# A fused attention and two-layer MoE kernel: the opening stretch put into a written order, with its loads on three queues

## The chip, the core and the metric

The kernel runs on one core of a Trainium2 chip. The metric is device time in microseconds (us), taken as the median of several executions of the compiled program. Before the change three runs gave 962.1, 963.79 and 965.07 us.

## What is computed

Attention, then a feed-forward layer with PReLU, then one with a rational function. The heads 0 to 3 look back 32 positions, the heads 4 to 7 look back 128 in steps of 4:

```python
batch, n_heads, seq, head_dim = (4, 8, 576, 64)
mask_plain = (rel >= 0) & (rel < window)                      # window = 32
mask_dil = (rel >= 0) & (rel < window * dilation) & (rel % dilation == 0)   # 4
scores = np.where(masks[None, :, :, :], scale * (q @ k.T), -1000000000.0)
attn = np.exp(scores - np.max(scores, axis=-1, keepdims=True))
attn = attn / (np.sum(attn, axis=-1, keepdims=True) + 1e-09)
x = attn @ v                                  # 2304 tokens x 512
h = x @ w_in                                  # 512 x 2048
x = (np.maximum(h, 0) + alpha * np.minimum(h, 0)) @ w_out     # 2048 x 512
h = x @ w_in2
P = a[0] + a[1]*h + a[2]*h*h + a[3]*h*h*h
Q = 1.0 + np.abs(b[0]) * np.abs(h) + np.abs(b[1]) * h*h
out = (P / (Q + 1e-06)) @ w_out2
```

The weights of the first layer reach the kernel as 64-bit floating point numbers, read as pairs of 32-bit words.

## The kernel before

The tokens go through the attention and the first layer in eight chunks of 288 (`u` = 0 to 7). A chunk has four attention jobs, one for each pair of heads `hp`: 0 and 1 plain, 2 and 3 dilated. A job is a Python generator; each `next` issues one of its steps. In order: load q and k; transpose them on PE into `pq` and `pk` (L382, L386); copy these to `qT` and `kT` on ACT (L392, L393); load v; scores `ps` on PE (L435 plain, L423 dilated); masked row maxima on DVE (L449), in two groups of blocks; exponentials with row sums on ACT (L457); normalize on DVE (L464, L465, L467); transpose the probabilities on PE into `pp` (L478); copy them to `pT` on ACT (L484); multiply with v into `px` (L529); copy to the layer's input `x1f` (L541).

The first layer runs, for each chunk, in 16 steps of 128 hidden features: `h` (L668 for the first 8 steps of chunk 0, in plain fp32; L551 for the rest, in three passes over a high and a low half), the PReLU on ACT and DVE (L685, L688, L691), which needs `side` and `salpha` made from `alpha` at L629 to L634, and the second product `y` (L716, L725). The trace's `h0`, `h1`, ... below are the steps 0, 1, ... of chunk 0.

The weights are decoded from their 64-bit form by turns. A turn loads a block of w_in and, from turn 2 on, one of w_out into one of two `raw` buffers (`w64_load`, L134 and L139; the turns 0 and 1 bring w_in alone), turns the exponent on ACT (L148), then sign, upper and lower part on DVE (L154, L161, L168; the last once for w_in and once for w_out). With two buffers the load of turn n waits for the decoding of turn n-2.

What stands ahead of the steady loop is the head: the four jobs of chunk 0, the first turns, and PE's warm-up matmuls (L606). The string `HEAD` lists it, one character a step: a digit is the next step of that job (0 to 3 counts in the order of `HPS`, so job 0 of the string is pair 1), `d`, `x`, `J`, `i`, `h`, `l` are the stages of the decoding, `k` starts the first job of chunk 1. The scheduler is free to choose another order within it. After it, attention jobs of the later chunks are put at fixed half steps of the loop, and `PACE` says how many turns of decoding each step takes along. Loads are issued by SP, in its program's order; `alpha`, `a` and `b` by POOL. An fp32 matmul leaves two records in the trace, so that a step `h` of four matmuls counts x8. In the rows a job of chunk 0 has the name `hd`, and later ones `tq`, `tk`, `tv`, `pr`, `pT`.

Of the kernel before, what the change touches and what calls it, by code (L numbers as in the profile page):

```python
# [22 lines left out]
def tile_attention_moe_moe2(  # L23
# [48 lines left out]
    HEAD = '0d12d30011xj01Ji223301h2300110011xj22223333Jil001101d22010331hlxj220133Ji012301d23k0123hl23xj2323Jidhl'  # L72
# [3 lines left out]
    MANH = ''  # L76
    HPS = (1, 0, 3, 2)
    POOLJ = ()
    SPLIT = True
# [7 lines left out]
    PACE = ((8, 0.75), (16, 0.25), (24, 0.75), (128, 0.22))  # L87
# [190 lines left out]
    def mem_head(nm, dil):  # L278

        if dil:  # L280
            at = {"tq": (0, 0), "tk": (0, 512), "tv": (1, 0), "qT": (1, 512),
                  "kT": (2, 0), "pT": (2, 416), "pr": (3, 0)}
        else:
            at = {"tq": (0, 0), "qT": (0, 384), "tv": (1, 0), "kT": (1, 640),
                  "tk": (2, 0), "pr": (2, 512), "pT": (3, 0)}
# [22 lines left out]
    def attention_job(mem, u, hp, bk, eng=nc.sync, split=False):  # L308
# [5 lines left out]
        first = t0 == 0  # L314
        if dil:
            nb, bq = 4, C1 // 4
            kw = bq if first else bq + W
# [3 lines left out]
            tk = mem("tk", [kw, 2, 4 * D])  # L321

            def load(t, src, back):
                n = t.shape[0]
                s0 = t0 if not back or first else t0 - 4 * W
                eng.dma_start(
                    t,
                    src[b, h0 : h0 + 2, s0 : s0 + 4 * n, :].rearrange(
                        "h (i r) d -> i h (r d)", r=4
                    ),  # L330
                )

            load(tq, q, False)
            load(tk, k, True)

            duo = lambda t, j: t[:, j // 2, (j % 2) * 2 * D : (j % 2 + 1) * 2 * D]
            q_rows, k_rows = bq, kw
        else:


            nb, bq = 3, 96
            groups = ((0, 1, 2), (3, 4))
            rows, span = P, 96
            back = 0 if first else W
            key = [max(0, QS * j - W + back) for j in range(5)]
            k_rows = 96 if first else 80
            nk = (C1 + back) // k_rows
            tq = mem("tq", [bq, nb, 2, D])
            tk = mem("tk", [k_rows, nk, 2, D])

            def load(t, src, s0, step, n):
                for h in range(2):
                    eng.dma_start(
                        t[:, :n, h, :],
                        bass.AP(
                            src.tensor, ((b * H + h0 + h) * S + s0) * D,
                            [[D, t.shape[0]], [step * D, n], [1, D]],
# [3 lines left out]
            def load_one(t, src, s0):  # L361

                eng.dma_start(
                    t,
                    bass.AP(
                        src.tensor, ((b * H + h0) * S + s0) * D,
                        [[D, t.shape[0]], [S * D, 2], [1, D]],
                    ),
                )

            load(tq, q, t0, bq, nb)
            load(tk, k, t0 - back, k_rows, nk)

            duo = lambda t, j: t[:, j].rearrange("p h d -> p (h d)")
            q_rows = bq
# [4 lines left out]
        kn = 4 if dil else nk  # L380
        for j in range(nb):
            nc.tensor.transpose(  # L382
                pq[:, j * q_rows : (j + 1) * q_rows], duo(tq, j), ident[:q_rows, :q_rows]
            )
        for j in range(kn):
            nc.tensor.transpose(  # L386
                pk[:, j * k_rows : (j + 1) * k_rows], duo(tk, j), ident[:k_rows, :k_rows]
            )
        yield
        kT = mem("kT", [P, kn * k_rows])  # L390
        qT = mem("qT", [P, C1])
        nc.scalar.activation(qT, pq[:, :C1], AF.Copy)  # L392
        nc.scalar.activation(kT, pk[:, : kn * k_rows], AF.Copy)  # L393
        yield
        if dil:
            tv = mem("tv", [kw, 2, 4 * D])
            load(tv, v, True)
        else:
            tv = mem("tv", [span, 5, 2, D])
            s0 = t0 - back  # L400
            if first:
                load_one(tv[:, 0], v, s0)
                load(tv[:, 1:], v, s0 + key[1], QS, 4)
            else:
                load(tv, v, s0, QS, 5)
# [8 lines left out]
        def scores():  # L414


            if dil:

                ps[:] = [bk(f"ps{nm}_{g}") for g in range(2)]
                for c in range(nb):  # L420
# [41 lines left out]
        def norm(gs):  # L462
            s = slice(groups[gs[0]][0], groups[gs[-1]][-1] + 1)
            nc.vector.tensor_scalar_add(sm[:, s], sm[:, s], 1e-9)  # L464
            nc.vector.reciprocal(sm[:, s], sm[:, s])  # L465
            n = s.stop - s.start
            (nc.vector if u < NORM_DVE else nc.gpsimd).tensor_tensor(  # L467
                pr[:, s], pr[:, s],
                sm[:, s].unsqueeze(2).to_broadcast([rows, n, span]), op=ALU.mult,
# [13 lines left out]
        def turned(g):  # L483
            nc.scalar.activation(  # L484
                pT[:, g * width[0] : g * width[0] + width[g]], pp[g][:span, : width[g]],
                AF.Copy,
            )
# [10 lines left out]
        if split:  # L498
            norm((0,))
            yield  # L500
# [3 lines left out]
        if split:  # L504
            turn(0)
            yield
            turned(0)
            yield
        rest = (1,) if split else (0, 1)
        norm(rest)  # L510
        yield
        for g in rest:
            turn(g)
        yield
        for g in rest:
# [539 lines left out]
```

## Time and profile before

| what | value |
|---|---|
| median of 3 runs | 963.79 us (962.1 to 965.07) |
| profiled execution | 964.02 us, of which span 962.2 us |
| mean granted clock of TensorE | 0.983 of full |
| PE busy | 936.0 us (97%) |
| DVE, ACT, POOL busy | 663.7 (69%), 631.8 (66%), 212.9 (22%) us |
| chain that ended last | PE 85%, DMA 5%, ACT 5%, DVE 3% |

The span is what the profiler saw from the first instruction to the last; the execution's own time is 1.8 us longer. PE is TensorE's matmuls, and PEclk its granted clock as a share of full speed, so 0.50 is the lower of its two levels (1.2 of 2.4 GHz). "Idle before" is the time an engine stood still just ahead of an instruction, and the name behind the arrow is what released it.

### The profile page before, as it was taken

To read this page: it belongs to the slowest core of one execution; us is meant where nothing else is said; L and a number is where in the kernel's file an instruction comes from. 1 tells how busy PE (TensorE), PEld (TensorE's weight loads), DVE (VectorE), ACT (ScalarE), POOL (GpSimd) and SP (SyncE) were. 2 spreads that over 40 slices of the span, in tenths; PEclk is the share of its full clock that TensorE was granted. 3 is DMA by queue.
4 is the path that set the end of the run, shared out by engine and by line. 5 is a ranking of instruction groups with operands and counts; after the bars stand their busy time and mean duration, and the time that the engine had idled before them with its cause. 6 is when DMAs were issued, how large, how long until landed. Compare 5 with 4: busy or idle time off the path is not lost.

```text
span 962.2 us, 18305 instructions
## 1 busy us (share of the span) xinstructions
PE 936.0 (97%) x6640; PEld 865.9 (90%) x6640; DVE 663.7 (69%) x1578; ACT 631.8 (66%) x1579; POOL 212.9 (22%) x257
## 2 busy tenths in 40 slices
PE   5899999999999999999999999999999999999998
PEld 5577998999999999999999999999999999999996
DVE  3688996556556555655536688877777777777776
ACT  3787676665564565555636588777776767767775
POOL 2000000010000010000013345443343343343332
PEclk7699999999999999999999999999999999999999
DMA  7655544463543544534144422021030020020000
GB/s 179 170 179 167 167 133 152 144 185 101 185 123 107 180 131 119 158 109 132 47 132 159 153 72 66 1 72 28 1 99 1 33 66 1 34 66 1 34 1 33
DMA packets 93898, 94.39 MB, mean 98 GB/s; under 512 B 40176, under 2 KB 81648, under 8 KB 93808
## 3 DMA queue, kind: packets, MB, share of 16 engines
q1 hardware_dynamic: 87360, 83.78, 28.5%
q0 software_dynamic: 6448, 9.45, 4.0%
q8 instruction: 52, 0.85, 0.4%
q14 instruction: 38, 0.31, 0.1%
HBM read 69.48 MB, written 23.72 MB: 97 GB/s over the span
## 4 chain that ended last, share of the span: by engine, by line
PE 85%; DMA 5%; ACT 5%; DVE 3%; issue 1%; SPq 0%; POOL 0%; POOLq 0%; ACTq 0%; DVEq 0%
PE h L551 39%; PE o L968 20%; PE y L725 17%; PE px L529 2%; DMA raw<-in_moe_w_out_dram 2%; DMA raw<-in_moe_w_in_dram 2%; PE pp L478 1%; PE ps L435 1%; PE h L668 1%; DMA hd<-in_q_dram 1%; PE ps L423 1%; ACT pr L457 1%; ACT hd L457 1%; PE y L716 1%; DMA x2hi<-y_0h 1%
## 5 line engine op out<-in xcount | busy, mean ns | idle before, releaser
L551 PE MATMUL h<-x1h,wl 128*128 128x288 f32 x480 | 147.2, 307 | 0.6 <-DVE g_9l L694 0.6
L551 PE MATMUL h<-x1l,wh 128*128 128x288 f32 x480 | 142.5, 297 | 0.0
L551 PE MATMUL h<-x1h,wh 128*128 128x288 f32 x480 | 142.0, 296 | 0.0
L688 DVE SCALAR_TENSOR_TENSOR h<-h,salpha,r 128x288 f32<-128x288 f32 x128 | 66.9, 523 | 95.2 <-ACT r L685 95.2
L551 PE MATMUL h<-x2h,wl 128*128 128x384 f32 x384 | 130.4, 340 | 0.0
L551 PE MATMUL h<-x2h,wh 128*128 128x384 f32 x384 | 130.0, 339 | 0.0
L551 PE MATMUL h<-x2l,wh 128*128 128x384 f32 x384 | 129.6, 338 | 0.0
L467 POOL TENSOR_TENSOR pr<-pr,sm 128x480 f32<-128x480 f32 (+2 forms) x20 | 23.9, 1197 | 453.4 <-DVE sm L465 384.7
L685 ACT ACTIVATE r<-h,side 128x288 f32<-128x288 f32 x128 | 63.7, 498 | 91.3 <-PE h L551 88.4
L900 POOL TENSOR_SCALAR qq<-hh,babs 128x384 f32<-128x384 f32 x96 | 56.7, 590 | 225.1 <-ACT hh L898 225.0
L903 POOL TENSOR_TENSOR qq<-qq,w 128x384 f32<-128x384 f32 x96 | 97.8, 1019 | 8.3 <-POOL qq L900 0.5
L551 PEld LDWEIGHTS h<-x1h,wl 128*128 128x128 f32 x480 | 90.5, 189 | 3.2 <-DVE g_9l L694 0.7
L551 PEld LDWEIGHTS h<-x1l,wh 128*128 128x128 f32 x480 | 90.8, 189 | 0.4 <-DVE x1l L543 0.2
L551 PEld LDWEIGHTS h<-x1h,wh 128*128 128x128 f32 x480 | 90.7, 189 | 0.1
L898 ACT ACTIVATE hh<-h 128x384 f32<-128x384 f32 x96 | 47.0, 490 | 62.6 <-PE h L551 62.6
L905 DVE TENSOR_TENSOR t<-h,t 128x384 f32<-128x384 f32 x96 | 53.5, 557 | 47.6 <-ACT t L904 47.1
L551 PEld LDWEIGHTS h<-x2h,wl 128*128 128x128 f32 x384 | 72.0, 188 | 4.0
L551 PEld LDWEIGHTS h<-x2l,wh 128*128 128x128 f32 x384 | 72.1, 188 | 3.6
L914 ACT ACTIVATE w<-qq 128x384 f32<-128x384 f32 (+1 forms) x98 | 50.8, 519 | 33.7 <-POOL qq L903 33.6
L551 PEld LDWEIGHTS h<-x2h,wh 128*128 128x128 f32 x384 | 72.0, 187 | 0.0
L922 DVE TENSOR_TENSOR qq<-qq,w 128x384 f32<-128x384 f32 (+1 forms) x98 | 54.4, 555 | 24.6 <-ACT w L917 24.3
L457 ACT ACTIVATE pr<-pr,mx 128x96 f32<-128x96 f32 (+2 forms) x182 | 65.1, 361 | 7.0 <-DVE mx L449 7.0
(379 smaller groups left out, 2568.9 us busy)
## 6 DMA issues: line engine op xcount, KB each, us to landing
raw<-in_moe_w_in_dram SPq DMA_DIRECT2D x32, 512.0 KB
raw<-in_moe_w_out_dram SPq DMA_DIRECT2D x32, 512.0 KB
w2f<-w SPq DMA_DIRECT2D x32, 256.0 KB
w<-w2f SPq DMA_DIRECT2D x16, 512.0 KB
x2h<-x2hi POOLq DMA_DIRECT2D x6, 768.0 KB, 5.2
x2l<-x2lo POOLq DMA_DIRECT2D x6, 768.0 KB, 7.0
out_dram<-o SPq DMA_DIRECT2D x15, 256.0 KB
tq<-in_q_dram SPq DMA_DIRECT2D x28, 72.0 KB
```

Source lines behind the costliest of these rows:

```text
L457: nc.scalar.activation(pr[:, j, :], pr[:, j, :], AF.Exp, scale=-1.0, bias=mx[:, j : j + 1], accum_out=sm[:, j : j + 1],)
L551: nc.tensor.matmul(ph[:, :n], lhsT=w_[:, c * P : (c + 1) * P], rhs=x_[:, c, :], start=(i == 0), stop=(i == 3 * KD - 1),)
L685: nc.scalar.activation(r, h, AF.Identity, scale=sg)
L688: nc.vector.scalar_tensor_tensor(h, h, sa, r, op0=ALU.mult, op1=ALU.max)
L725: nc.tensor.matmul(ys[c][:, :C1], lhsT=w_[:, s], rhs=g_, start=begin and i == 0, stop=end and i == 2,)
L898: nc.scalar.activation(hh, h, AF.Square)
L900: nc.gpsimd.tensor_scalar(qq, hh, babs, 1.0 + 1e-6, op0=ALU.mult, op1=ALU.add)
L903: nc.gpsimd.tensor_tensor(qq, qq, w, op=ALU.add)
L905: nc.vector.tensor_tensor(t, h, t, op=ALU.mult)
L914: nc.scalar.activation(w[:, s], qq[:, s], AF.Abs_reciprocal_sqrt, scale=2.0**-44)
L922: nc.vector.tensor_tensor(qq[:, s], qq[:, s], w[:, s], op=ALU.mult)
L968: nc.tensor.matmul(o2[c][i], lhsT=g_, rhs=w_, start=(f == 0 and j == 0), stop=(f == NF - 1 and j == 2),)
```

## The change

The string `HEAD` is new, and the head is now always issued in exactly that order (`tc.manual_schedule()`), job by job, each engine's steps where their inputs are due. Along with it:

- q and k of chunk 0's jobs are loaded by SP for two of the jobs and by ACT's queue for the other two, v by POOL's queue.
- `alpha`, `a`, `b` and the three operations on them become a step of their own (`a`), late in the head.
- In the head the `kT` copies and the first half of the `pT` copies go to DVE; the exponentials no longer make the row sums, which a reduction on DVE does; the normalization is one for all blocks and no longer by groups.
- Three turns of weights are decoded within the head, before it was four; five are loaded, as before.
- `PACE` of the first 8 steps rises from 0.75 to 0.85.

The core of the diff:

```diff
-    HEAD = '0d12d30011xj01Ji223301h2300110011xj22223333Jil001101d22010331hlxj220133Ji012301d23k0123hl23xj2323Jidhl'
+    HEAD = (
+        '0123dd01010101000001111232212033322220010021333312132xjJid21'
+        '2323hlxjJid333hlaxjJidkhl'
+    )
...
-    PACE = ((8, 0.75), (16, 0.25), (24, 0.75), (128, 0.22))
+    PACE = ((8, 0.85), (16, 0.25), (24, 0.75), (128, 0.22))
...
+        load(tq, q, t0, eng)
+        load(tk, k, t0 - back, eng)
...
+        if head:
+            nc.vector.tensor_copy(kT, pk[:, : nk * kw])
+        else:
+            nc.scalar.activation(kT, pk[:, : nk * kw], AF.Copy)
...
+            load(tv, v, t0 - back, eng_v)
...
-                    pr[:, j, :], pr[:, j, :], AF.Exp, scale=-1.0,
-                    bias=mx[:, j : j + 1], accum_out=sm[:, j : j + 1],
-                )
...
+                    pr[:, j, :], pr[:, j, :], AF.Exp, scale=-1.0, bias=mx[:, j : j + 1],
+                    **({} if head else dict(accum_out=sm[:, j : j + 1])),
+                )
...
+            if head:
+                nc.vector.tensor_reduce(
+                    out=sm, in_=pr, op=ALU.add, axis=mybir.AxisListType.X
+                )
...
+            t = pT[:, g * width[0] : g * width[0] + width[g]]
+            if head and g == 0:
+                nc.vector.tensor_copy(t, pp[g][:span, : width[g]])
+            else:
+                nc.scalar.activation(t, pp[g][:span, : width[g]], AF.Copy)
...
+                0, hp, hb, (nc.sync, nc.scalar)[i % 2], nc.gpsimd, True,
+            )
+            for i, hp in enumerate(HPS)
...
+                elif s == "a":
+                    sides()
...
-        if MANH:
-            with tc.manual_schedule():
-                head()
-        else:
+        with tc.manual_schedule():
             head()
```

What the change moves, at three places. On PE, around the first steps of the layer, before (`px` and `ps` of chunk 0 and of the first job of chunk 1 carry the job's number; `h_0_0` is step 0, `h_0_1` step 1; `pq_0_493`, `pk_0_494` and `ps_0_512` belong to chunk 1):

```order
L529 MATMUL px_3_444<-hd_3_2_102,hd_3_1_101 64x72 x6
L668 MATMUL h_0_0_609<-x1f,w_0_195 128x288 x2
L529 MATMUL px_2_453<-hd_2_2_106,hd_2_1_105 64x72 x6
L382 MATMUL pq_0_493<-ident,tq_0_420 128x96 x3
L668 MATMUL h_0_0_609<-x1f,w_0_195 128x288
L386 MATMUL pk_0_494<-ident,tk_0_421 128x80 x4
L668 MATMUL h_0_0_609<-x1f,w_0_195 128x288
L668 MATMUL h_0_1_674<-x1f,w_1_309 128x288
L435 MATMUL ps_0_512<-kT_0_502,qT_0_503 64x96 x10
L668 MATMUL h_0_1_674<-x1f,w_1_309 128x288 x3
L668 MATMUL h_0_2_719<-x1f,w_2_382 128x288 x4
```

and after it:

```order
L477 MATMUL pp_2_1_410<-ident,hd_2_3_107 72x72 x4
L661 MATMUL h_0_0_598<-x1f,w_0_383 128x288 x3
L520 MATMUL px_2_426<-hd_2_2_106,hd_2_1_105 64x72 x8
L661 MATMUL h_0_1_663<-x1f,w_1_419 128x288
L661 MATMUL h_0_0_598<-x1f,w_0_383 128x288
L661 MATMUL h_0_1_663<-x1f,w_1_419 128x288 x3
L661 MATMUL h_0_2_717<-x1f,w_2_446 128x288 x4
```

The first job of chunk 1 no longer stands between the steps 0 and 1; its `pq` and `pk` come within the second half of `y` of step 1, and its `ps` after that, ahead of step 4.

On DVE, the third and fourth job's ends and the first two turns of decoding, after the change (`w_0` and `w_1` are the turns 0 and 1):

```order
L485 COPY hd_0_3_99<-pp_0_0_329 96x384
L462 TENSOR_REDUCE sm_3_257<-hd_3_3_103 72x8
L465 TENSOR_SCALAR sm_3_257<-sm_3_257 72x8
L466 RECIPROCAL sm_3_257<-sm_3_257 72x8
L467 TENSOR_TENSOR hd_3_3_103<-hd_3_3_103,sm_3_257 72x576
L154 TENSOR_SCALAR w_0_380<-raw_157 128x512
L161 SCALAR_TENSOR_TENSOR w_0_380<-raw_157,w_0_380 128x512
L168 SCALAR_TENSOR_TENSOR w_0_383<-raw_157,w_0_380 128x512
L485 COPY hd_3_2_102<-pp_3_0_369 72x288
L462 TENSOR_REDUCE sm_2_276<-hd_2_3_107 72x8
L465 TENSOR_SCALAR sm_2_276<-sm_2_276 72x8
L466 RECIPROCAL sm_2_276<-sm_2_276 72x8
```

Before, turn 0 was decoded ahead of every row maximum of the head, and turn 1 too; now both stand behind all 26 of them.

On SP, the sixth turn's two loads (`raw_642`), after the change:

```order
L139 DMA raw_449<-in_moe_w_out_dram 128x1024
L352 DMA tq_0_452<-in_q_dram 96x3x64 x2
L352 DMA tk_0_453<-in_k_dram 80x4x64 x2
L134 DMA raw_642<-in_moe_w_in_dram 128x4x256
L352 DMA tq_1_520<-in_q_dram 96x3x64 x2
L352 DMA tk_1_521<-in_k_dram 80x4x64 x2
L139 DMA raw_642<-in_moe_w_out_dram 128x1024
```

Before, the two loads of that turn stood next to each other; now the q and k of chunk 1's second job are between them. The eighth turn's halves have the `tk` of the fourth job between them, where before the seventh's had `tq` and `tk` of the third.

## Rows read from the trace of the kernel before

**Rows 1.** Page, section 1: busy time, share and instructions of each engine.

```profile
PE 936.0 (97%) x6640; PEld 865.9 (90%) x6640; DVE 663.7 (69%) x1578; ACT 631.8 (66%) x1579; POOL 212.9 (22%) x257
```

**Rows 2.** Busy time by stretch (us, length, busy us per engine, PEclk, DMA share, GB/s).

```profile
24.00:36.00 12.00, 8.86 (x87) 6.60 (x88) 8.96 (x41) 11.26 (x47) 0.00 (x0) 0.65 0.68 182
36.00:48.00 12.00, 10.96 (x57) 7.42 (x58) 6.25 (x19) 6.13 (x18) 0.00 (x0) 0.63 0.56 160
...
72.00:96.00 24.00, 21.71 (x143) 17.50 (x142) 20.08 (x48) 18.11 (x49) 0.00 (x0) 0.93 0.57 166
96.00:120.00 24.00, 24.00 (x182) 23.72 (x182) 23.09 (x36) 16.40 (x31) 0.00 (x0) 1.00 0.51 167
120.00:962.00 842.00, 833.73 (x5875) 780.32 (x5874) 577.44 (x1329) 552.43 (x1352) 208.00 (x240) 1.00 0.29 88
```

**Rows 3.** Timeline of PE: start us, length us, line, names, count [idle before, releaser].

```profile
1.60 5.49 PE L606 MATMUL warm<-ident 128*128 128x128 f32 x24 [1.60 <-POOL ident masks.py:199]
...
13.44 0.74 PE L386 MATMUL pk<-ident,hd 96*128 96x96 f32 x3 [4.82 <-DMA hd<-in_k_dram]
...
17.14 0.74 PE L382 MATMUL pq<-ident,hd 72*128 72x72 f32 x4 [1.92 <-DMA hd<-in_q_dram]
...
24.74 0.88 PE L478 MATMUL pp<-ident,hd 128*96 128x128 f32 x6 [2.14 <-ACT hd L457]
...
35.74 2.29 PE L668 MATMUL h<-x1f,w 128*128 128x288 f32 x4
...
38.88 0.74 PE L382 MATMUL pq<-ident,tq 96*128 96x96 f32 x3
...
43.10 1.83 PE L435 MATMUL ps<-kT,qT 64*64 64x96 f32 x20
...
47.62 2.21 PE L668 MATMUL h<-x1f,w 128*128 128x288 f32 x8 [1.04 <-ACT g_0h L691]
```

**Rows 4.** Single microseconds, same columns as rows 2: the granted clock.

```profile
43.00:44.00 1.00, 1.00 (x13) 0.90 (x14) 0.37 (x1) 0.04 (x1) 0.00 (x0) 0.50 0.78 178
...
45.00:46.00 1.00, 1.00 (x5) 0.79 (x6) 1.00 (x11) 0.72 (x4) 0.00 (x0) 1.00 0.95 313
86.00:87.00 1.00, 1.00 (x7) 0.86 (x4) 0.01 (x1) 0.70 (x1) 0.00 (x0) 0.50 0.12 45
...
89.00:90.00 1.00, 1.00 (x5) 0.81 (x5) 1.00 (x3) 0.75 (x2) 0.00 (x0) 0.93 0.00 1
```

**Rows 5.** Timeline of DVE: first row maximum of the plain pairs, first of the dilated.

```profile
20.36 0.26 DVE L449 CUSTOM_DVE_ANT_0 hd<-ps,masks 128x96 f32<-128x96 f32 x1 [1.11 <-PE ps L435]
...
22.36 0.22 DVE L449 CUSTOM_DVE_ANT_0 hd<-ps,masks 72x72 f32<-72x72 f32 x1
```

**Rows 6.** Groups of DVE, 0 to 50 us: busy us, mean ns, idle before.

```profile
L168 DVE SCALAR_TENSOR_TENSOR w<-raw,w 128x512 int32<-128x512 int32 x8 | 5.3, 685 | 0.1
L161 DVE SCALAR_TENSOR_TENSOR w<-raw,w 128x1024 int32<-128x1024 int32 x3 | 3.7, 1223 | 0.1
...
L467 DVE TENSOR_TENSOR pr<-pr,sm 128x480 f32<-128x480 f32 x1 | 0.7, 654 | 0.0
```

**Rows 7.** Groups of ACT, 0 to 50 us, same columns.

```profile
L148 ACT ACTIVATE raw<-raw 128x1024 f32<-128x1024 f32 x3 | 3.3, 1116 | 0.0
...
L393 ACT ACTIVATE hd<-pk 128x288 f32<-128x288 f32 x4 | 1.7, 435 | 0.0
```

**Rows 8.** Timeline of SP: the issue of the third turn of weights.

```profile
18.07 0.39 SPq L134 DMA_DIRECT2D raw<-in_moe_w_in_dram  x1
```

**Rows 9.** DMA issues, 0 to 90 us: count, KB each, median us from issue to landing.

```profile
alpha_sb<-in_moe_alpha_dram POOLq DMA_DIRECT2D x1, 8.0 KB, 7.7
```

**Rows 10.** Waits of PE, 34 to 100 us: total us, times, longest us.

```profile
PE px L529 <- ACT pT L484: 2.3, 1, 2.3
PE pq L382 <- ACT pT L484: 1.1, 1, 1.1
PE h L668 <- ACT g_0h L691: 1.0, 1, 1.0
```

More of the change, by code (lines that the diff above doesn't have):

```diff
@@ L305, in mem_head, with attention_job @@
         return f
-    def attention_job(mem, u, hp, bk, eng=nc.sync, split=False):
+    def attention_job(mem, u, hp, bk, eng=nc.sync, eng_v=nc.sync, head=False):
         b, t0 = divmod(u * C1, S)
@@ L314, in attention_job @@
         first = t0 == 0
+        back = 0 if first else (4 * W if dil else W)
         if dil:
-            nb, bq = 4, C1 // 4
-            kw = bq if first else bq + W
+            nq = nk = 4
+            bq = C1 // 4
+            kw = bq + back // 4
             groups = ((0, 1, 2, 3), (4, 5, 6, 7))
@@ L321, in attention_job, with load @@
             tk = mem("tk", [kw, 2, 4 * D])
-            def load(t, src, back):
-                n = t.shape[0]
-                s0 = t0 if not back or first else t0 - 4 * W
+            duo = lambda t, j: t[:, j // 2, (j % 2) * 2 * D : (j % 2 + 1) * 2 * D]
+            def load(t, src, s0, eng):
                 eng.dma_start(
                     t,
-                    src[b, h0 : h0 + 2, s0 : s0 + 4 * n, :].rearrange(
+                    src[b, h0 : h0 + 2, s0 : s0 + 4 * t.shape[0], :].rearrange(
                         "h (i r) d -> i h (r d)", r=4
@@ L396, in attention_job @@
             tv = mem("tv", [kw, 2, 4 * D])
-            load(tv, v, True)
+            load(tv, v, t0 - back, eng_v)
         else:
@@ L400, in attention_job @@
             s0 = t0 - back
+            n1 = 1 if first else 0
             if first:
-                load_one(tv[:, 0], v, s0)
-                load(tv[:, 1:], v, s0 + key[1], QS, 4)
-            else:
-                load(tv, v, s0, QS, 5)
+                eng_v.dma_start(
+                    tv[:, 0],
+                    bass.AP(
+                        v.tensor, ((b * H + h0) * S + s0) * D,
+                        [[D, span], [S * D, 2], [1, D]],
+                    ),
+                )
+            for h in range(2):
+                eng_v.dma_start(
+                    tv[:, n1:, h, :],
+                    bass.AP(
+                        v.tensor, ((b * H + h0 + h) * S + s0 + key[n1]) * D,
+                        [[D, span], [QS * D, 5 - n1], [1, D]],
+                    ),
+                )
         yield
@@ L419, in scores @@
                 ps[:] = [bk(f"ps{nm}_{g}") for g in range(2)]
-                for c in range(nb):
+                for c in range(4):
                     for g in range(2):
@@ L503, in attention_job @@
         pT = mem("pT", [span, sum(width)])
[L504 to L510, printed above, removed]
+        norm()
         yield
-        for g in rest:
+        for g in range(2):
             turn(g)
         yield
-        for g in rest:
+        for g in range(2):
             turned(g)
@@ L599, in tile_attention_moe_moe2 @@
                 mem_head(f"0_{hp}", 2 * hp >= H // 2),
-                0, hp, hb, nc.gpsimd if hp in POOLJ else nc.sync, SPLIT,
+                0, hp, hb, (nc.sync, nc.scalar)[i % 2], nc.gpsimd, True,
             )
-            for hp in HPS
+            for i, hp in enumerate(HPS)
         ]
```

90 lines of the change are left out of this document (29 added, 61 removed).

## The prediction

> **What bounds the kernel now.** I read the page first: PE is busy 97% of the span [rows 1]. Then the busy time by stretch: from 96 us on PE stands still for 8 us in 866 [rows 2]. So whatever the opening gains or loses arrives undiminished at the end, unless it is gone by 96 us, and nothing behind that needs a term. The sum is made against the profiled execution, 964.02 us with a span of 962.2; the median of the three runs, 963.79, is 0.2 us lower, which I neglect. About 0.3%, 2.9 us, is what a measurement of this kernel can tell from no change.
>
> Third, PE's timeline for the opening. The warm-up ends at about 7 us. Then PE waits 4.82 us for the k of the second plain job and 1.92 us for a q, and its first matmul of the layer, h of step 0, starts at 35.74 us; step 2 starts at 47.62 [rows 3]. Fourth, the granted clock: 0.50 while 43 to 44 us, 1.00 from 45 on, 0.50 again at 86 to 87, and back by the end of 89 to 90 [rows 4]. Last, PE's waits between 34 and 100 us: three, of 2.3, 1.1 and 1.0 us [rows 10].
>
> **1. The head gets shorter: -8.7 us.** q and k of two jobs leave SP's list, where a turn of weights stood ahead of them, and are issued by ACT at the start; the waits of 4.82 and 1.92 us [rows 3] go, since loads that start at 1 us have the warm-up to hide under. What is late next is DVE, which now has a chain of work from the first `pk` (7.5 us) to the last normalization ahead of h: four `kT` copies at 0.44, ACT's price for them [rows 7], 1.7 us; 26 row maxima, of which ten took 2.0 us [rows 5], so at most 5.2, I take 4.7; four sums of 480 or 576 elements, a kind that DVE does not show, at the price of the product over 480, 0.65 [rows 6], and in proportion 0.78 for 576, 2.9 us; four normalizations, such a product each and two small operations of about 0.2, 4.4 us; three `pT` copies at about 0.45, 1.3 us; and turn 0's decoding, three operations of at most 0.69 [rows 6], 1.9 us. Together 17 us, so 24.5 us without a gap. DVE will wait for the exponentials in a few places; I take 2 us for these and 0.5 for the last `pp`, and have h of step 0 at 27 us, 8.7 earlier. The ends are 25 us (no gap, -10.7) and 31 us, if the gaps are as in the head of before, where `pp` began at 24.74 and h only 11.0 us later [rows 3] (-4.7). The exponentials without sums free ACT, which is not what ends this chain; they cost nothing. PE's clock does not matter here, since PE waits for DVE.
>
> `alpha`'s late use is covered too: it landed 7.7 us after its issue [rows 9], and behind the v's on POOL that is still before 27 us. Were it not, the PReLU of step 0 would wait, and h of step 2 with it.
>
> **2. From step 0 to step 2: +0.3 us.** Before, 11.9 us lay between the starts of the two [rows 3], with `pq`, `pk` (0.74 each at half clock) and `ps` (1.83) of the next chunk among them and 1.04 of waiting. After, these three stand behind `y` of step 1 and take about half there, 1.7 us. The two steps themselves are 16 records, 9.2 us at the 2.29 for four [rows 3], and the last `px` of the head 1.0: 10.2 us at half clock. 10.2 + 1.7 - 11.9 is 0. At full clock it would be 5, but then the weights of step 2 are late: turn 2 can be issued only when DVE has decoded turn 0, at about 23.5 us in the chain above, where before it was issued at 18.07 [rows 8]. One megabyte takes 3.4 us at 313 GB/s [rows 4], an estimate without what starts a transfer; then 1.1 on ACT [rows 7], behind the copy of the last `px` (about 31 us), and on DVE 0.69 + 1.22 + 0.69 [rows 6] with two PReLU operations of 0.5 between. Step 2 thus cannot start before 36 us, and at half clock it would start at 37 or 38. Both lead to much the same; I add 0.3 for an inner wait at `px`.
>
> **3. The clock: +2 us.** Before, the half clock ended at 45 us, when step 1 was nearly done. [...] The nearest rows are those of the second fall: PE had just waited 2.3 us, the clock was half at 86 to 87, PE worked without a break, and the clock was full within 89 to 90 [rows 4, 10]. I take it to go alike here after step 2's wait: it rises at about 41 us instead of 37, and 4 us at half rate lose 2. Ends: 0, when it has risen before, and +5, when it rises only after the dense small matmuls of `ps`, as it did before, which now stand ten microseconds further on.
>
> **4. Weights behind q and k: +3 us.** The second halves of the turns 5 and 7 are issued after loads of q and k whose buffers wait for PE. Their `y` products come two steps after h, but both halves are decoded in one go, so h of the steps 5 and 7 is late as well. I take 1.5 us each, between the 1.0 and 2.3 of the waits that the trace shows [rows 10]; ends 0 and 4.6 together.
>
> **5. Attention of chunk 1 in a shorter space: +2.8 us.** The first job of chunk 1 starts behind step 1 and not in step 0, so its round trips PE, ACT, DVE, ACT, DVE, PE, ACT, PE have less matmul work to hide under, and the other jobs follow. I count six places where PE waits (its first two `ps`, a `pp`, the `pq` of the third job, and two around the last `px`), at 1.0 to 1.2 us each, the two smaller waits of [rows 10], 6.2 us; this takes the place of 3.4 us (2.3 and 1.1) of before. Ends -3.4 and +10. The clock's second fall, which cost about half of 3.5 us, I leave in.
>
> **6. `PACE` and the rest: 0.** A quicker pace moves decoding forward by part of a step in the first eight; DVE is busy for 8.96 of 12 us and 20.08 of 24 us in the stretches of [rows 2], so there is room, though no more than a fifth. The head decodes one turn fewer, the pace returns it. If the room is missing, that is term 4.
>
> Sum: -8.7 + 0.3 + 2 + 3 + 2.8 = -0.6, 963.4 us. I forecast **no change that can be told, 963.5 us**, with 961 to 966.9 as this case's own range.
>
> **The queues, by the row and by a rule.** The k that PE waited for until 13.4 us stood on SP's list behind the first turn of weights and two q's [rows 3]; I take it that being first in line is what helps. The Trainium skill, page "DMA: Bandwidth & Descriptors", section "Issuing engines are not separate DMA queues", says that loads issued by several engines share the same sixteen DMA engines and interleave, so that only the sequencer's time is saved. By it the loads that are moved to ACT's and POOL's queues slow the ones that stay, and only the order among them helps; no run here shows which of the two it is.
>
> **The rivals.**
>
> *Faster, 957.8 us, chance 0.27.* The weights and the round trips of chunk 1 keep up: terms 4 and 5 are 0. Then -8.7 + 0.3 + 2 + 0 + 0 is -6.4 and, with the small waits rounded, 957.8. For it: ACT was busy for 18.11 and DVE for 20.08 us of 24 in the stretch from 72 us [rows 2], so neither is full. Against it: the waits that exist today are of this kind [rows 10], with more cover.
>
> *Slower, 968.6 us, chance 0.22.* The h matmuls in fp32 do not raise the clock by themselves. Before, h of step 0 had PE busy without a gap from 35.74 us, and yet the clock was half at 43 to 44, and it was full only once `ps` of chunk 1 had begun at 43.10 [rows 3, 4]. That `ps` now stands behind `y` of step 1. The half clock would last from 27 to about 48 us, not 41, and a fall after the wait of step 7 costs another 1.7: 3.5 + 1.7 on top of the sum, +4.6. It decides at the place of `ps`: when the clock is still half at 44 us, this rival is right. Against it: the rise at 89 us came while large matmuls alone ran.
>
> *The loads share what they had, 967.4 us, chance 0.08.* Three streams at once bring q and k of the first jobs in turns, the plain k lands after the warm-up, and the first `ps` waits up to the 4.82 us of before; of these 4 reach h of step 0, -0.6 + 4. This is the rule of the Trainium skill named above, at its strongest. Against it: q and k of the two plain pairs are 0.59 MB (four times 288 x 128 x 4 bytes), 3.2 us at the 182 GB/s of [rows 2], which the warm-up covers.
>
> That the change does not do what it says is hardly open: the order is fixed by the program.
>
> **How the numbers follow.** The forecast has 0.38, the three rivals 0.27, 0.22 and 0.08, and 0.05 is left for cases outside them, 0.03 faster and 0.02 slower. So faster by over 0.3% has 0.30, within it 0.38, slower 0.32. The range from 957 to 970 takes in all four cases with the nearer ends of their terms (the gapless head for the faster one, a half microsecond more at each wait for the slower) and leaves out about 0.2 beyond them.
>
> **What would show it.** In the profile of the changed kernel: h of step 0 near 27 us (25 to 31), no wait for `hd` loads after the warm-up (term 1, and the third rival); step 2 at 36 to 38 us (term 2); the granted clock at 1.00 by 41 us (term 3; still 0.50 at 44, the second rival); waits ahead of h of the steps 5 and 7 whose chain leads to L148 and a load of w_out (term 4); and some 6 us of waits for ACT's and DVE's attention steps between 40 and 90 us (term 5; under 2, the first rival). PE should be busy without a gap from about 96 us as before. The prediction is wrong if that steady part has waits of its own, or if h starts later than 31 us.

## The result, and the profile after

The changed kernel took 967.18 us (median of 8 runs, 965.59 to 973.4), the kernel before beside it 962.84 (8 runs, 961.38 to 965.07): a ratio of 1.0052, 95% interval 1.0029 to 1.0074. It is **slower by half a per cent**, 4.3 us, where no change was forecast.

The profiled execution of the changed kernel is its fastest, 965.59 us with a span of 963.6, and that of before, 964.02, is one of its slower ones; the spans of the two traces differ by 1.4 us and the medians by 4.3. Lengths of single stretches are therefore compared between traces, and ends between medians.

PE's timeline of the changed kernel, to be held against [rows 3]:

```profile
1.61 4.56 PE L597 MATMUL warm<-ident 128*128 128x128 f32 x24 [1.61 <-POOL ident masks.py:199]
...
25.05 3.18 PE L661 MATMUL h<-x1f,w 128*128 128x288 f32 x6
...
34.34 2.34 PE L661 MATMUL h<-x1f,w 128*128 128x288 f32 x7 [2.12 <-DVE w L168]
```

The first matmul of the layer starts at 25.05 us and not at 35.74, and step 2 at 34.34 and not at 47.62: a lead of 10.7 and of 13.3 us. The waits for k and q are gone. PE's waits from 26 to 96 us (total, times, longest):

```profile
PE h L661 <- DVE w L168: 4.4, 2, 2.3
PE ps L433 <- ACT kT L378: 1.7, 2, 1.1
PE pk L368 <- ACT qT L374: 0.7, 1, 0.7
```

The two waits of h for its weights are step 2 (2.1 us) and step 7 (2.3 us). The granted clock in single microseconds (columns as in [rows 4]):

```profile
28.00:29.00 1.00, 1.00 (x17) 0.84 (x16) 0.00 (x0) 0.00 (x0) 0.00 (x0) 0.55 0.89 262
29.00:30.00 1.00, 0.90 (x10) 0.37 (x6) 0.00 (x0) 0.73 (x2) 0.00 (x0) 1.00 1.04 367
37.00:38.00 1.00, 1.00 (x4) 0.71 (x3) 1.00 (x2) 0.50 (x1) 0.00 (x0) 0.50 1.11 386
71.00:72.00 1.00, 1.00 (x8) 0.97 (x7) 1.00 (x3) 0.72 (x3) 0.00 (x0) 0.50 0.27 43
324.00:325.00 1.00, 1.00 (x6) 1.00 (x5) 0.15 (x1) 0.61 (x1) 0.68 (x1) 0.50 0.54 161
```

It came back within 28 to 29 us, fell again after each of the two waits, and, where nothing had been expected, once more near 322 us. Busy time by stretch, against [rows 2]:

```profile
24.00:36.00 12.00, 9.69 (x47) 6.69 (x48) 7.59 (x16) 5.36 (x10) 0.00 (x0) 0.78 0.44 159
36.00:48.00 12.00, 11.47 (x62) 8.82 (x61) 7.19 (x19) 5.38 (x16) 0.00 (x0) 0.87 0.78 205
48.00:72.00 24.00, 19.86 (x156) 14.66 (x155) 19.95 (x58) 20.19 (x60) 0.00 (x0) 0.96 0.58 192
72.00:96.00 24.00, 22.89 (x182) 18.59 (x181) 22.17 (x52) 20.70 (x53) 0.00 (x0) 0.97 0.68 201
96.00:120.00 24.00, 24.00 (x183) 24.00 (x182) 23.09 (x46) 17.20 (x40) 0.00 (x0) 1.00 0.47 160
120.00:962.00 842.00, 830.18 (x5821) 776.40 (x5819) 573.29 (x1314) 546.25 (x1333) 208.07 (x240) 1.00 0.29 87
```

From 96 to 120 us PE is full in both kernels. But in the last row it is busy for 830.18 us where it had been busy for 833.73. PE's waits from 96 us to the end, after:

```profile
PE y L718 <- DVE y_3l L749: 2.8, 3, 1.8
PE pp L477 <- DVE pr L467: 2.1, 2, 1.9
PE pp L477 <- POOL pr L467: 1.5, 3, 0.6
PE px L520 <- DVE mx L447: 1.3, 1, 1.3
PE y L718 <- DVE yp L745: 1.1, 1, 1.1
```

and before:

```profile
PE pp L478 <- DVE pr L467: 1.5, 1, 1.5
PE y L725 <- DVE y_3l L756: 0.9, 2, 0.7
PE h L551 <- DVE g_9l L694: 0.6, 1, 0.6
PE pp L478 <- POOL pr L467: 0.6, 2, 0.3
```

All of PE's waits there come to 9.3 us after and 4.0 before. As one mark I use the start of the 241st three-pass matmul of h (L551 before, L542 after), near 155 us; up to it PE has done the same matmuls in every kernel here. Before and after:

```profile
160.60 0.40 PE L551 MATMUL h<-x1h,wl 128*128 128x288 f32 x1
```

```profile
153.87 0.40 PE L542 MATMUL h<-x1h,wl 128*128 128x288 f32 x1
```

That is a lead of 6.7 us. From the mark to the end of the span it is 801.6 us before and 809.7 after. **The lead was there, and 8.1 us were lost behind it**: PE's waits from 96 us on are 5.3 us longer, and the half clock of 3.4 us at 322 us costs 1.7, half of its length. (Held against the medians the lead is about 4 us, an estimate: 1.2 us less for the trace of before and 1.6 less for that of the changed kernel. 8.1 less that is the 4.3 us by which the medians differ, if the loss is the same in every execution.)

### The profile page after: what moved, and what is told of

The parts are those of the page before. It is cut to its first block, busy times and chain, and to the rows that moved or that the text cites. A ratio compares the mean times of both kernels' runs of the same rounds, so it can differ in the third digit from the quotient of the medians.

```text
span 963.6 us, 18292 instructions
## 1 busy us (share of the span) xinstructions
PE 933.7 (97%) x6640; PEld 862.9 (90%) x6640; DVE 669.0 (69%) x1578; ACT 627.4 (65%) x1545; POOL 218.5 (23%) x265
## 4 chain that ended last, share of the span: by engine, by line
PE 79%; DVE 6%; DMA 5%; ACT 4%; issue 1%; POOL 0%; SPq 0%; POOLq 0%; ACTq 0%; DVEq 0%
PE h L542 37%; PE o L961 20%; PE y L718 15%; DMA raw<-in_moe_w_out_dram 3%; PE px L520 1%; PE pp L477 1%; PE y L709 1%; DVE w L161 1%; ACT pr L455 1%; DVE w L168 1%; PE ps L421 1%; PE h L661 1%; DVE h L681 1%; DMA raw<-in_moe_w_in_dram 1%; DVE w L154 1%
## 5 line engine op out<-in xcount | busy, mean ns | idle before, releaser
L542 PE MATMUL h<-x1h,wl 128*128 128x288 f32 x480 | 146.5, 306 | 0.4 <-ACT x1h L532 0.4
L542 PE MATMUL h<-x1l,wh 128*128 128x288 f32 x480 | 142.6, 297 | 0.0
L542 PE MATMUL h<-x1h,wh 128*128 128x288 f32 x480 | 141.8, 295 | 0.0
L542 PE MATMUL h<-x2h,wl 128*128 128x384 f32 x384 | 130.4, 340 | 0.0
L542 PE MATMUL h<-x2h,wh 128*128 128x384 f32 x384 | 130.0, 339 | 0.0
L542 PE MATMUL h<-x2l,wh 128*128 128x384 f32 x384 | 129.6, 338 | 0.0
L542 PEld LDWEIGHTS h<-x1h,wl 128*128 128x128 f32 x480 | 90.4, 189 | 3.0 <-ACT x1h L532 0.6
L542 PEld LDWEIGHTS h<-x1l,wh 128*128 128x128 f32 x480 | 90.7, 189 | 0.3 <-DVE x1l L534 0.2
L542 PEld LDWEIGHTS h<-x1h,wh 128*128 128x128 f32 x480 | 90.6, 189 | 0.1
L542 PEld LDWEIGHTS h<-x2h,wl 128*128 128x128 f32 x384 | 72.0, 188 | 4.0
L542 PEld LDWEIGHTS h<-x2l,wh 128*128 128x128 f32 x384 | 72.1, 188 | 3.6
L542 PEld LDWEIGHTS h<-x2h,wh 128*128 128x128 f32 x384 | 72.0, 187 | 0.0
```

Source lines behind the costliest of these rows:

```text
L542: nc.tensor.matmul(ph[:, :n], lhsT=w_[:, c * P : (c + 1) * P], rhs=x_[:, c, :], start=(i == 0), stop=(i == 3 * KD - 1),)
```

## The experiments

All runs in one table, so that the two parts can be read apart: when step 0's first matmul starts, the mark, the length from the mark to the end (all three from the profiled execution), the median of the runs, and its ratio to before, whose runs beside it differ a little from row to row, with the 95% interval. "Turns" is how many turns of weights are decoded by step 8: those in the head and what the pace adds in the eight steps.

| kernel | turns | step 0 | mark | mark to end | median | ratio |
|---|---|---|---|---|---|---|
| before | 10.0 | 35.7 | 160.6 | 801.6 | 962.84 | 1 |
| changed | 9.8 | 25.0 | 153.9 | 809.7 | 967.18 | 1.0052 (1.0029 to 1.0074) |
| 1 changed, pace 0.875 | 10.0 | 24.8 | 155.6 | 801.6 | 960.66 | 0.9986 (0.9969 to 1.0003) |
| 2 before, pace 0.725 | 9.8 | 36.5 | 158.4 | 803.2 | 963.27 | 1.0013 (1.0001 to 1.0025) |
| 3 changed, pace 0.9 | 10.2 | 25.0 | 159.0 | 808.0 | 969.25 | 1.0079 (1.0054 to 1.0104) |
| 4 before, pace 0.775 | 10.2 | 37.2 | 159.6 | 801.2 | 959.59 | 0.9973 (0.9954 to 0.9992) |
| 5 changed, ACT of step 66 in program order | 9.8 | 25.2 | 158.4 | 813.8 | 972.00 | 1.0094 (1.0059 to 1.0129) |
| 6 changed, one queue | 9.8 | 32.3 | 163.2 | 809.2 | 972.63 | 1.0109 (1.0092 to 1.0127) |
| 7 changed, alpha first | 9.8 | 32.9 | 162.3 | 806.7 | 972.30 | 1.0103 (1.0088 to 1.0118) |
| 8 as 1, one queue, alpha late on it | 10.0 | 25.1 | 163.7 | 801.8 | 970.77 | 1.0085 (1.0053 to 1.0118) |
| 9 as 1, alpha's load first, its use late | 10.0 | 29.8 | 163.2 | 802.2 | 965.98 | 1.0033 (1.0015 to 1.0051) |
| 10 before, three queues | 10.0 | 42.2 | 162.8 | 801.8 | 966.53 | 1.0053 (1.0031 to 1.0074) |
| 11 as 10, alpha behind the first v | 10.0 | 40.3 | 160.4 | 801.7 | 966.02 | 1.0040 (1.0021 to 1.0058) |
| 12 as 1, DVE's new work back on ACT | 10.0 | 28.4 | 158.1 | 802.1 | 961.46 | 0.9998 (0.9980 to 1.0016) |
| 13 as 1, turn 0 decoded earlier | 10.0 | 27.2 | 159.1 | 802.5 | 963.64 | 1.0022 (1.0003 to 1.0041) |
| 14 as 1, pace 1.0 then 0.75 | 10.0 | 25.2 | 154.1 | 802.7 | 960.97 | 0.9989 (0.9971 to 1.0006) |
| 15 as 1, pace 1.0 then 0.5 | 10.0 | 27.4 | 158.9 | 804.2 | 962.21 | 0.9996 (0.9977 to 1.0015) |

### The loss behind the mark: the place of the decoding turns (1 to 4)

The old head decoded four turns and its pace of 0.75 added 6.0 in eight steps; the new one decodes three and its 0.85 adds 6.8. Ever after, the turns come 0.2 of a turn later.

```diff
-    PACE = ((8, 0.85), (16, 0.25), (24, 0.75), (128, 0.22))
+    PACE = ((8, 0.875), (16, 0.25), (24, 0.75), (128, 0.22))
```

> The changed kernel with the pace of the first eight steps at 0.875 in place of 0.85, so that with three turns decoded in the head it has decoded 10.0 turns by step 8, as the kernel before, and not 9.8. Theory A (the turns of decoding fall into other half steps of the steady loop and delay attention steps and copies there): the head's lead of about 5 us at 120 us stays as it is, PE's waits between 120 and 560 us fall from 9.5 to about 4 us and the half-clock stretch at 322 us goes; 959 to 962 us, faster than before by 1 to 4 us. Theory B (the waits come with the order that the scheduler writes for the steady loop, which any change of the head reshuffles, whatever the phase): waits between 6 and 11 us at other places, 963 to 969 us.

```diff
-    PACE = ((8, 0.75), (16, 0.25), (24, 0.75), (128, 0.22))
+    PACE = ((8, 0.725), (16, 0.25), (24, 0.75), (128, 0.22))
```

> The kernel before with the pace of the first eight steps at 0.725 in place of 0.75, so that 9.8 turns are decoded by step 8 as in the changed kernel; its head is unchanged. Theory A: no lead at 120 us, and waits between 120 and 560 us of some 9 us in place of 4: 967 to 970 us. Theory B: waits anywhere from 3 to 8 us, 962 to 967 us.

Run 1 keeps the head's lead and has no loss: 801.6 us behind the mark, waits of 3.2 us between 115 and 560, no half clock at 322; 6.5 us less than the changed kernel by the medians. Theory A forecast that. Run 2 speaks against it in its plain form: the old head at 9.8 turns pays 1.6 us, not 6. The other side was tried as well, with 0.9 for the new head and 0.775 for the old one:

> The changed kernel with the pace of the first eight steps at 0.9: 10.2 turns decoded by step 8. If the loss in the steady loop belongs to turns that fall onto the ends of chunks because they come late (9.8 turns), there is none here: PE's waits between 115 and 560 us at 3 to 5 us, the stretch from 155 us to the end 801 to 803 us as with 10.0 turns. If any departure from 10.0 costs, waits of 6 to 10 us and 804 to 810 us.

> The kernel before with the pace of the first eight steps at 0.775: 10.2 turns by step 8. With the changed head 10.2 turns made the stretch from the 241st three-pass matmul of h to the end 808.0 us long in place of 801.5. If that belongs to the place of the turns, it takes 804 to 810 us here too; if the changed head is needed for it, 801 to 803.5 us, as at 9.8 turns with this head (803.2).

10.2 turns cost the new head 6.4 us behind the mark and the old head nothing. So neither the place of the turns nor the new head makes the loss by itself; **both together do**: at 10.0 turns all ten kernels but one, of either head, lie between 801.6 and 802.7 us (run 15 has 804.2, with 3.4 us of half clock), and the changed head away from 10.0 lies between 806.7 and 813.8.

These are fewer cases than rows. Behind the mark the traces show one and the same order of instructions in before and the runs 10 and 11, one in run 1 and its followers (8, 9, 12 to 15), and one in the changed kernel and the runs 6 and 7. What is compared is thus one written order for each head at each sum of turns, six in all, and run 5's. Between the heads at equal turns these orders differ little: of DVE's some 1,250 instructions behind the mark 10 stand elsewhere at 10.0 turns, 28 at 9.8 and 6 at 10.2. Another sum of turns moves more: 85 from run 1 to the changed kernel, 71 from before to run 2. PE's order does not part so clearly (98 matmuls between the heads at 9.8 turns, 77 from run 1 to the changed kernel). Both thus move the order, on DVE the turns more, and few places decide whether PE waits. That any new head would lose so away from 10.0 turns is not shown.

What it looks like in one place, ACT's timeline of the changed kernel at the end of chunk 3, with the copies of the four quarters of y (`y_0h` to `y_3h`, L748):

```profile
314.44 0.40 ACT L748 ACTIVATE y_0h<-y 128x288 fp32r<-128x288 f32 x1
...
315.02 0.42 ACT L748 ACTIVATE y_2h<-y 128x288 fp32r<-128x288 f32 x1
...
318.62 0.76 ACT L487 ACTIVATE pT<-pp 96x384 f32<-96x384 f32 x2 [1.81 <-PE pp L477]
320.66 0.38 ACT L455 ACTIVATE pr<-pr,mx 128x96 f32<-128x96 f32 x1 [1.28 <-DVE mx L447]
...
321.75 0.39 ACT L748 ACTIVATE y_3h<-y 128x288 fp32r<-128x288 f32 x1
```

The first three are done by 315.4 us. Between them and the fourth stand, in the order that the scheduler wrote, the attention's qT, kT, pT and four exponentials and an operation of the PReLU; the fourth comes at 321.75, and PE, whose next y waits for DVE's operation behind it (L749), has stood for 1.75 us:

```profile
322.69 0.61 PE L718 MATMUL y<-g_0h,wl 128*128 128x288 f32 x1 [1.75 <-DVE y_3l L749]
```

In run 1 the fourth copy comes 3.4 us behind the third, behind the exponent of a turn (L148) whose load ACT awaits for 1.70 us, and no y of PE waits for it. There the turn of weights was issued on SP 4.1 us ahead of `y_0h`, and in the changed kernel 0.1 us behind it. The changed kernel's SP, then run 1's SP and its ACT:

```profile
314.52 0.40 SPq L134 DMA_DIRECT2D raw<-in_moe_w_in_dram  x1
```

```profile
307.16 0.40 SPq L134 DMA_DIRECT2D raw<-in_moe_w_in_dram  x1
```

```profile
311.25 0.40 ACT L748 ACTIVATE y_0h<-y 128x288 fp32r<-128x288 f32 x1
...
315.26 0.40 ACT L748 ACTIVATE y_3h<-y 128x288 fp32r<-128x288 f32 x1
```

Can it be mended where it shows? Run 5 has ACT keep the program's order in that step, and moves `y_3h` ahead of the attention's work:

```diff
-    MAN = ''
-    MAN_FROM = 0
-    MAN_TO = 128
+    MAN = 'A'
+    MAN_FROM = 66
+    MAN_TO = 67
```

> The changed kernel (pace 0.85) with ACT's instructions of one step of the loop, step 66, in the order in which the program writes them. Of the kernel's 32 chunk-end copies this puts the one of chunk 3's last quarter ahead of the attention's pT copies and exponentials that the scheduler had put before it; some ten rows of ACT change place and a few of PE and DVE next to them. Theory C (that place of the copy makes PE wait 1.75 us at 322 us and lets the clock fall): the wait and the half-clock stretch at 322 us go, and the end comes 3 to 4 us earlier, 963 to 964.5 us; the other waits (163, 186, 272 us) stay. Theory D (the loss is spread over DVE and decoding, and this wait only moves): less than 1.5 us, 966 to 968 us.

It got worse, outside what either theory had. ACT's timeline of run 5 and PE's:

```profile
325.04 1.10 ACT L148 ACTIVATE raw<-raw 128x1024 f32<-128x1024 f32 x1 [5.26 <-DMA raw<-in_moe_w_out_dram]
326.05 0.39 ACT L748 ACTIVATE y_3h<-y 128x288 fp32r<-128x288 f32 x1
```

```profile
326.99 0.61 PE L718 MATMUL y<-g_0h,wl 128*128 128x288 f32 x1 [4.93 <-DVE y_3l L749]
```

In the program's order the exponent of the next turn (L148) stands ahead of `y_3h`, and its load, issued at the wrong moment, kept ACT for 5.26 us. Theory C has the place right, since PE's wait follows the copy, but the remedy exchanged one predecessor for a worse one, so it does not show what the copy alone was worth. This wait is 3.2 us longer than in the changed kernel, and the half clock behind it lasts 6.8 us and not 3.4; 3.4 us of half clock near 169 us, ahead of the edited step, are not its doing. In run 3 it is yet another place: PE waits for a load of k, and the clock falls behind it for 6.8 us, which together are 5.8 of the 6.4 us that run 3 loses:

```profile
166.93 0.44 PE L368 MATMUL pk<-ident,tk 72*128 72x72 f32 x4 [2.35 <-DMA tk<-in_k_dram]
```

### What made the head shorter: the place of alpha, not the queues (6 to 11)

```diff
-                0, hp, hb, (nc.sync, nc.scalar)[i % 2], nc.gpsimd, True,
+                0, hp, hb, nc.sync, nc.sync, True,
```

> The changed kernel with all loads of q, k and v of the head's jobs issued by SP. If the three queues are what shortens the head, the first step of the layer starts 3 to 5 us later than its 25.0 us, and the lead at 120 us is 0 to 2 us in place of 5; the end then lies between 967 and 972 us. If the order of the loads does it (q and k ahead of the weights), the first step starts within 1 us of 25 us and the lead at 120 us stays at 4 to 5 us.

```diff
-        '0123dd01010101000001111232212033322220010021333312132xjJid21'
-        '2323hlxjJid333hlaxjJidkhl'
+        'a0123dd01010101000001111232212033322220010021333312132xjJid21'
+        '2323hlxjJid333hlxjJidkhl'
```

> The changed kernel with the load of alpha, a and b and the operations on them put at the start of the head in place of its end. If alpha's load slows the loads beside it, the first step of the layer starts 1 to 4 us later than 25.0 us; if it is hidden anyway, within 0.5 us. In either case the lead at 120 us changes by less than 2 us, and the end lies at 964 to 970 us, depending on what the steady loop's order becomes.

Each lost the lead, 7.2 and 7.8 us at step 0, more than either expectation had allowed. But run 6 mixes two causes: with no v ahead of it on POOL, alpha was issued at 3.3 us, as in run 7 and in the kernel before, and not at 8.9 as in the changed one. And in run 7 it was DVE that stood, for alpha's landing, ahead of all its other work:

```profile
11.60 0.17 DVE L627 TENSOR_SCALAR side<-alpha_sb 128x16 f32<-128x16 f32 x1 [11.60 <-DMA alpha_sb<-in_moe_alpha_dram]
```

Two more runs, at pace 0.875, take these apart. In run 8 the loads of alpha, a and b go to SP as well (`nc.sync` for `nc.gpsimd` in `sides`); in run 9 they are a step of their own at the start of `HEAD`, and the DVE operations stay late.

> The changed kernel at pace 0.875 with every load of the head issued by SP, in the order of the program, and alpha, a and b there too, behind the loads of turn 3. In the run with one queue and alpha on POOL the first step started at 32.3 us, but POOL, with nothing ahead of it, had issued alpha at 3.3 us, so two causes were mixed. If the queues are the cause, the first step still starts at 30 to 33 us and the end is 964 to 968 us. If alpha's early load is the cause, it starts at 25 to 28 us and the end is 958 to 963 us.

> The changed kernel at pace 0.875 with the loads of alpha, a and b at the start of POOL's list, but the three DVE operations on alpha left late. In the run with both early DVE stood for alpha until 11.6 us. If DVE's wait was the cause of the late first step there (32.9 us), it now starts at 25 to 27 us; if alpha's load holds back the other loads, v above all, which now stand behind it on POOL, at 29 to 33 us.

Run 8, PE's timeline:

```profile
25.07 3.18 PE L661 MATMUL h<-x1f,w 128*128 128x288 f32 x6
...
36.55 3.70 PE L661 MATMUL h<-x1f,w 128*128 128x288 f32 x7 [4.44 <-DVE w L168]
```

With one queue and alpha late, step 0 starts at 25.07 us, as with three queues: **the queues shorten nothing**. (Run 8 loses its lead later: behind turn 3's loads alpha was too late, DVE waited for it until 32.6 us, and step 2 waited 4.44; so its end missed the expected 958 to 963 us.) With alpha early and used late, step 0 starts at 29.8 us, 4.9 later than in run 1. The first `pk` comes 1.3 us later there, and the v's stand behind alpha, so that PE waits for one:

```profile
19.26 1.11 PE L520 MATMUL px<-hd,hd 96*64 96x56 f32 x14 [1.89 <-DMA hd<-in_v_dram]
```

Alpha's load is 2,048 pieces of four bytes; a and b, which are small too, go with it. In run 6 k landed late beside them:

```profile
10.89 0.71 PE L368 MATMUL pk<-ident,hd 96*128 96x96 f32 x3 [3.25 <-DMA hd<-in_k_dram]
```

The half clock follows this wait: the 40 `ps` behind it take 3.47 us, where they take 1.87 in the changed kernel. All the loads were slow while alpha was under way. From 6 to 8 us, run 6 and then run 8, which issues the same loads on the same queue without alpha, a and b (the last two columns are the DMA engines' share and GB/s):

```profile
6.00:8.00 2.00, 1.63 (x15) 1.45 (x13) 0.46 (x1) 0.74 (x2) 0.00 (x0) 1.00 0.58 68
```

```profile
6.00:8.00 2.00, 1.85 (x33) 1.70 (x33) 0.92 (x2) 0.82 (x2) 0.00 (x0) 1.00 0.69 187
```

So 4.9 to 7.8 us of the 10.7 at step 0 hang on alpha's place. The rest belongs to the other edits, of which only the moves to DVE are taken apart below; the order of q and k ahead of the weights, the order of the steps and the new places of the head's buffers, which the diff moves too (`tk`, `qT`, `pr`), were not undone one at a time. The queues, put into the kernel before, made it slower:

> The kernel before with one part of the change alone: q and k of the head's jobs by SP and ACT in turns, v by POOL behind alpha. If the queues give the head its lead, PE's waits of 4.82 and 1.92 us for k and q go and the first step starts 3 to 6 us earlier than 35.7 us; the end is at 957 to 960 us. If alpha, which still goes first on POOL, holds v up, the first step starts within 2 us of 35.7 us, and the end lies at 961 to 964 us.

> As the run before, with alpha, a and b issued on POOL behind the first job's v. If alpha's load is what holds the others up, the first step starts 2 to 5 us earlier than with alpha first, near 29 to 32 us, and the end is at 955 to 959 us; if it does not matter, the two agree within 1 us.

There alpha still went first, or second, on POOL's list with v behind it, and with q and k gone from its list SP took loads of chunk 1 in their place; step 0 came 6.4 and 4.6 us later than before. Both expectations missed, with the wrong sign.

### Inside the head (12 to 15)

Run 12 takes the three moves of work to DVE back (`nc.scalar.activation` for both copies, `accum_out` in every exponential, no reduction).

> The changed kernel at pace 0.875 with the three moves of work from ACT to DVE in the head undone: kT copies and the first half of the pT copies on ACT, sums from the exponentials, no reduction on DVE. If DVE's chain is what sets the start of the first step, as the prediction's term 1 has it, about 6 us of DVE work go and that start comes 1 to 4 us earlier than 24.8 us, unless ACT, with 4 us of sums and 3 us of copies more, takes its place: then it comes 0 to 3 us later. The steady loop keeps its order, so the end moves with it: 957 to 963 us.

Step 0 comes 3.5 us later; the end, 961.46 us against 960.66, is too near to tell. PE's waits name ACT's copies:

```profile
PE px L510 <- ACT hd L477: 2.3, 1, 2.3
PE ps L418 <- ACT hd L375: 2.1, 1, 2.1
```

Run 13 moves `xjJid`, turn 0's decoding, in the string ahead of the nine steps `333312132`.

> The changed kernel at pace 0.875 with turn 0's decoding and the load of turn 2 behind it moved ahead of the last two jobs' row maxima and products. By the prediction's term 2 step 2's wait for its weights (2.1 us) comes from turn 2's load, issued at 21.9 us; it should be issued some 4 us earlier and the wait and the half clock after it (35 to 39 us) go, while the first step starts up to 1.9 us later: step 2 at 32 to 35 us, the end 0 to 3 us earlier than the 960.7 us of that pace. If step 2 is bound by something else, its start moves back with the first step and the end is 0 to 2 us later.

Step 0 came 2.4 us later, and step 2 still waited 1.8 us for its weights; step 2 was not sooner but 4 us later. The runs 14 and 15 take the turns 3 to 7 earlier:

```diff
-    PACE = ((8, 0.875), (16, 0.25), (24, 0.75), (128, 0.22))
+    PACE = ((4, 1.0), (8, 0.75), (16, 0.25), (24, 0.75), (128, 0.22))
```

> The changed kernel with the pace of the first eight steps at 1.0 for four of them and 0.75 for four: 10.0 turns at step 8 as with 0.875, but the turns 3 to 7 are taken along up to half a step earlier. If step 7 waits (2.3 us, and the clock falls behind it) because its turn of weights is late, the wait shrinks or goes, the half clock at 69 us with it, and the end is 1 to 4 us earlier than the 960.7 us of the even pace: 957 to 960 us. If the wait comes from DVE and ACT being filled by attention, it stays within 0.5 us or grows: 960 to 963 us.

> As the run before with the pace at 1.0 for six steps and 0.5 for two, so that turn 7 is another half step earlier. If lateness is the cause, step 7's wait is gone and the end is 956 to 960 us; if DVE and ACT are full there, other waits of PE between 45 and 80 us take its place, together 4 us and more as before, and the end is 960 to 964 us.

In run 14 step 7's wait for weights is gone, 2.5 us in run 1. Its waits from 26 to 110 us:

```profile
PE ps L433 <- ACT kT L378: 2.7, 3, 1.1
PE h L661 <- DVE w L168: 2.1, 1, 2.1
PE pq L368 <- ACT pT L487: 1.4, 1, 1.4
PE pp L477 <- DVE pr L467: 1.4, 2, 1.1
```

`ps` waits for kT and `pq` for ACT's pT instead, step 7 starts at 70.5 us and not at 69.1, the clock falls at 70 us all the same, and the end is where it was. From 60 to 72 us DVE is busy for 11.0 and ACT for 10.5 of the 12 us; a turn that comes earlier seems to push attention back. In run 15 `pq` waits 2.8 us for pT, and its end, 962.21 us, is within the 960 to 964 expected for that case.

## Why the prediction was wrong

**Term 1, the head: right in kind, too small, and its cause was wrong.** Step 0 started at 25.05 us, the gapless end of the range given (27 was taken, -8.7; it was -10.7). DVE's chain was the bound: it ran from 6.7 to 24.0 us with 1.0 us of gaps, where 2.5 had been taken. But I had credited the order of q and k ahead of the weights for the waits that went, and called alpha's place covered, as a cost that could only appear. With q and k ahead of the weights an early alpha still makes PE wait 3.25 us for k (run 6), and with a late one the wait is gone (run 8); whether the order helps besides, no run shows. And the moves from ACT to DVE, booked as a pure cost of 6 us on DVE, are worth 3.5 us at step 0 (run 12): without them PE waits for ACT's copies.

**Term 2 held**: 9.3 us from step 0 to step 2 against 10.2, with the wait for turn 2's weights in it (2.1 us).

**Term 3 held in its sign, full clock by 41 us, and not in its size; the second rival fell.** The clock was full by 29 us, long before any `ps` of chunk 1; it fell after step 2's wait and was back before 40 us. That the clock stays half through the first two steps, as the sum takes it, is not what the trace shows: from step 0 to 50 us the clock was half for 7.3 us, where before it was half for 9.1, so the clock gave back about 0.9 us, part of it in term 2's stretch, and did not cost 2.

**Term 4 was half right.** Step 7 waited 2.3 us, step 5 not at all. The chain of step 7 does lead to a load of w_out, issued at 58.2 us and landed at 63.1, behind which the exponent begins. But DVE then took until 69.0 us for that turn, with attention's work in between, so a late load alone was too simple a reading: with the turn earlier the wait changes its place (runs 14 and 15).

**Term 5 was too large.** PE stood 5.8 us from 36 to 96 us (from the rows by stretch), where the terms 4 and 5 had 9.2. Of that step 7 is 2.3; the 3.5 left for attention are no more than the 3.4 that they replace, where 6.2 had been counted.

So the opening came out better than forecast: the lead at the mark is 6.7 us in the profiled executions, the sum had 0.6. How much of it would reach the end, run 1 shows, which keeps the lead and loses nothing behind the mark: 960.66 us, 2.0 below the before beside it (962.7) and not told from it. With the steady loop as it was, no change that can be told would have come out, though not for the terms given; the first rival's 957.8 would not. The third rival's 967.4 lies next to the measured 967.18 by luck: PE waited for no load of `hd` after the warm-up, so its cause did not occur.

**The step that failed** is the first: "from 96 us on PE stands still for 8 us in 866", so that "nothing behind that needs a term". That row says that the steady loop of before is full; it does not say that the loop stays the same. The change altered it through term 6, which booked the pace at 0 because "the pace returns it": of the one turn taken from the head the pace returns 0.8, the turns by step 8 went from 10.0 to 9.8, and the scheduler wrote another order of the steady loop, one in which PE waits. That cost 8.1 us in the profiled execution; with 10.0 turns and the same head the loss is gone (run 1). My sign for what would prove me wrong, "if that steady part has waits of its own", is what happened.

**The rule on queues**, cited from the Trainium skill, page "DMA: Bandwidth & Descriptors", section "Issuing engines are not separate DMA queues", says that loads issued by several engines share the same sixteen DMA engines. The runs agree: one queue and three give step 0 at 25.07 and 24.85 us (runs 8 and 1), with alpha behind the v's in both.

What stays open: why 9.8 and 10.2 turns cost the new head 6 us and more and the old one 1.6 us or nothing. The places of three of the losses were seen (the copy of y, the exponent behind a late load, a load of k), not why the scheduler puts them so for this head. Of the 8.1 us, about 1 is in neither the waits nor the half clock. Each length behind the mark is from one execution.

The fastest version run is the kernel before at a pace of 0.775: 959.59 us, 0.9973 of before (0.9954 to 0.9992), with its old head. The new head at 10.0 turns, 960.66, is not told from before at 95%, though it is 6.5 us below the changed kernel.

## What to carry to other kernels

A change in the head of a loop that a scheduler orders can be a change of the whole loop: count what it does to the rhythm of everything that is taken along at a rate (here the sum of turns by a fixed step), try it with that sum kept equal, and compare the length behind a fixed mark. When a bundle of edits moves loads, undo them one at a time and look at what else was moved by the undoing: "one queue" had also brought alpha to the front. Here a small load of scattered elements did best behind the large ones, issued early enough that its first use did not wait.

## What the runs showed of the hardware

A load of 8 KB in pieces of four bytes, with the two small ones of a and b, held back the loads beside it: 68 GB/s with them (run 6) and 187 without (run 8), from 6 to 8 us, while the share of the DMA engines was 0.58 and 0.69.

Waits of PE of about 2 us were sometimes followed by a stretch of half clock and sometimes not: 1.75 us at 322.7 us was, 1.94 at 162.9 in the same trace was not, and a wait of 2.3 us at 167 in run 5 was. Run 5 has the same instructions in the same order as the changed kernel up to about 310 us. There step 2 waited just as long, and the clock stayed full behind it, where it fell in the changed kernel:

```profile
34.51 1.69 PE L661 MATMUL h<-x1f,w 128*128 128x288 f32 x6 [2.12 <-DVE w L168]
```

Run 5 yet reached the mark 4.5 us later, with half clock for 6.8 us at 70 us (3.4 in the changed kernel) and for 6.8 more at 87: 6.8 us more of half clock in all, which is 3.4 of the 4.5 us. So much can two executions of one program differ by the clock's falls.
